# Block scaling and column shares of chunks three and four on VectorE instead of GpSimd, in a planned DeltaNet and SwiGLU kernel

## Chip, core and metric

The kernel runs on one core of one Trainium2 chip. The metric is the device time of one execution in microseconds, as the median of three runs.

## What is computed

The reference is a DeltaNet recurrence over 768 time steps for 4 batches and 8 heads of width 48, followed by an RMS norm and a SwiGLU feed-forward on the 3072 tokens of width 384 (inner width 1536):

```python
k_n = k / (np.linalg.norm(k, axis=-1, keepdims=True) + 1e-06)
for t in range(S):
    kt, vt, bt = (k_n[:, :, t], v[:, :, t], beta[:, :, t, None])
    y[:, :, t] = np.einsum('bhd,bhde->bhe', q[:, :, t], state)
    v_old = np.einsum('bhde,bhd->bhe', state, kt)
    state = state + bt[:, :, :, None] * np.einsum('bhd,bhe->bhde', kt, vt - v_old)
...
rms = np.sqrt(np.mean(x * x, axis=-1, keepdims=True) + 1e-06)
xn = x / rms * rms_g
g = xn @ w_gate
silu = g * (1.0 / (1.0 + np.exp(-g)))
val = xn @ w_val
return (silu * val @ w_out).astype(np.float32)
```

The weights arrive as 64-bit floats and are converted to 32 bits in the kernel.

## The kernel before

Time is cut into 12 chunks of 64 steps (`NCH`; `c` counts from 0, so the third and fourth chunk are `c = 2` and `c = 3`). Inside a chunk the recurrence needs the inverse of a unit triangular matrix of size 64 per head. `prep(c)` builds it from 32 x 32 blocks, 128 of them side by side, one per partition:

- the products of the keys (L537) are copied to SBUF (L634), stored to DRAM (`dkk`) and loaded back in another layout, one block per partition (`at`, L645);
- `scale` (L651) multiplies `at` by beta, a 128 x 1024 operation with two SBUF inputs;
- `share1` (L676), `share3` (L686, two small ones) and `share2` (L681) add to each odd column its share of the even one before it;
- 15 steps on VectorE (L698 multiply, L704 reduce) substitute forward two columns at a time in `acc`;
- the result is spread by copies (L721 on ScalarE, from the third chunk on also L725 on GpSimd), goes through DRAM (`dx`, `dxt`) and comes back as `mt`, `x2bd` and `m1bd`; two small products (L780, L804) finish `mt`.

For the first two chunks (`early`) the scaling and the shares run on VectorE, for the other ten on GpSimd; that is what `eng, e_` in L595 chooses. GpSimd also does the power operations (L559, L991, L992) and the scaling of keys (L626).

`recur(c)` then does the recurrence of a chunk: products on the state (L845), with the residual by VectorE (L859), `mt` times residual (L891), copied to `u` by VectorE (L930) and ScalarE (L928), then L905 and L942, sums (L973, L1044), the norm (L979 to L1007) and the transposes L1013. The feed-forward of the first two chunks (`ffn_plain`) has 12 column blocks in four passes, 24 in all: two products per block (L1080), Silu on ScalarE (L1087), the multiplication on VectorE that also empties the PSUM bank (L1088), and the product down (L1062). From the third chunk on `ffn` uses 15 products per half in place of 18 (L1173, L1183 to L1190) and a down product of the same kind (L1230). These need sums of weights, which VectorE makes once (L1136, L1138, L1209) after the 18 weight loads have been converted (L464 on ScalarE, L452, L455, L460 and L485 on VectorE).

Nothing of this is issued in the order of the code. Every piece is an operation of `Plan`: an engine, a duration, a priority, and the keys that it reads and writes. `Plan.run` plays the operations forward with these durations, and backward for new priorities, 60 times with some random shaking, and issues the order of the best round: each engine's queue is then fixed, and the engines meet only in semaphores. `op.port` (L87) makes the plan keep VectorE and GpSimd operations on SBUF apart. DMAs have a release time `after` in the plan, before which it doesn't start them; it is used in planning only. Up to 70 us of the plan, `filler` puts matmuls on a spare bank (L1330) where PE would stand idle. A changed duration, engine or release time can so change the order of every engine.

Of the kernel before, what the change touches and what calls it, by code (L numbers as in the profile page):

```python
# [248 lines left out]
def kernel(  # L249
# [17 lines left out]
    nc = tc.nc  # L267
# [24 lines left out]
    bk = sbt("bk", [128, W])  # L292
# [13 lines left out]
    NK, NKQ = 3, 2  # L306
    k2 = sbt("k2", [128, 16, DP], NK)
    q2 = sbt("q2", [128, 16, DP])
    vt = sbt("vt", [128, 16, D])
# [14 lines left out]
    acc = sbt("acc", [128, 4, W // 2, W])  # L324
# [21 lines left out]
    raw = [more[:, 1536 * i : 1536 * i + 1536].bitcast(I64) for i in range(NRAW)]  # L346
# [11 lines left out]
    P = Plan()  # L358
# [5 lines left out]
    def dma(dst, src, prio, r=(), w=(), work=0.3, dur=0.5, eng="SP", after=0.0):  # L364
        queue = nc.scalar if eng == "ACT" else nc.sync
        op = P.add(eng, dur, lambda: queue.dma_start(out=dst, in_=src), prio, r, w, lat=0.7)
        op.dma, op.work, op.ready = True, work, after
# [55 lines left out]
    def weights():  # L423
        todo = []
        for half_ in range(2):
            c0 = half_ * WCOL

            for i_ in range(3):
                for side, (key, w) in enumerate((("wg", moe_w_gate), ("wv", moe_w_val))):
                    c1 = c0 + 256 * i_  # L430
                    src = w.rearrange("(t p) c -> p t c", p=128)[:, :, c1 : c1 + 256]
                    todo.append((w_in[:, side, half_, i_:9:3], src, [(key, half_, i_)]))
                if i_:
                    for f in ((6 * half_,) if i_ == 1 else (6 * half_ + 2, 6 * half_ + 4)):
                        src = moe_w_out[f * 128 : f * 128 + 256, :].rearrange("(a p) c -> p a c", a=2)
                        z = spot(f)
                        todo.append((wo_sb[:, z : z + 2], src, [("wo", f), ("wo", f + 1)]))
        for n, (dst, src, keys) in enumerate(todo):
            pr = (30 if n < 9 else CV2) + 0.2 * n
            i, a = n % NRAW, n % NCV  # L440
            parts = dst.shape[1]
            rdst = raw[i].rearrange("p (a c) -> p a c", a=parts)
            dma(rdst, src, (0.1 if n == 0 else 3 + 2 * n), w=[("raw", i)], dur=0.7, work=3.06, after=(7.5, 5.0, 19.2, 27.2, 18.7, 33.3, 47.0)[n] if n < 7 else 48.8)

            low, high = (raw[i].bitcast(U32)[:, w_ : w_ + 2 * WCOL - 1 : 2] for w_ in range(2))
            top, cc = cva[a], cvb[a]
            u = top.bitcast(U32)
            tiled = lambda t: t.rearrange("p (a n) -> p a n", a=parts)
            cak, cvk = [("cva", a)], [("o", 1)] if a else [("tmp", 1), ("tmp", 2)]

            def s2(u=u):
                nc.vector.tensor_scalar(out=u, in0=u, scalar1=3, scalar2=None, op0=ALU.logical_shift_left)  # L452

            def s4(u=u, cc=cc):
                nc.vector.tensor_scalar(  # L455
                    out=cc.bitcast(U32), in0=u, scalar1=0xFF800000, scalar2=None, op0=ALU.bitwise_and
                )

            def s5(low=low, cc=cc, by=2.0**-52):
                nc.vector.scalar_tensor_tensor(out=cc, in0=low, scalar=by, in1=cc, op0=ALU.mult, op1=ALU.mult)  # L460

            P.add("ACT", 0.84, lambda high=high, top=top: nc.scalar.activation(out=top, in_=high.bitcast(FP32), func=ACTF.Prelu, scale=2.0**-112, alpha=2.0**32), pr, r=[("raw", i)], w=cak)  # L464
            P.add("DVE", 0.57, s2, pr, w=cak)
            P.add("DVE", 0.57, s4, pr, r=cak, w=cvk)
            P.add("DVE", 0.96, s5, pr, r=[("raw", i)], w=cvk)
            done = []
            if n < NPE:
                for x_ in range(2):  # L470
                    ps = Group()
                    cut = slice(2 * x_, 2 + x_)
                    flat = slice(512 * x_, 512 + 256 * x_)
                    m = 512 - 256 * x_

                    def s6(ps=ps, top=top[:, flat], cc=cc[:, flat], m=m):
                        nc.tensor.matmul(ps.t[:, 0:m], ident, top, start=True, stop=False)
                        nc.tensor.matmul(ps.t[:, 0:m], ident, cc, start=False, stop=True)

                    P.add("PE", 0.0035 * m, s6, pr, r=cvk + cak + ["ident"], w=[("cvp", n, x_)], ps=ps, size=8)  # L480
                    done.append(("cv", n, x_))
                    P.add("ACT", A(m), lambda dst=dst[:, cut], ps=ps, m=m: nc.scalar.copy(dst, ps.t[:, 0:m].rearrange("p (a n) -> p a n", n=256)), pr, r=[("cvp", n, x_)], w=[done[-1]], last=ps)
            else:
                done.append(("cv", n))
                P.add("DVE", 0.97, lambda dst=dst, top=tiled(top), cc=tiled(cc): nc.vector.tensor_tensor(out=dst, in0=top, in1=cc, op=ALU.add), pr, r=cvk + cak, w=[done[-1]])  # L485
            for key in keys:
                ready.setdefault(key, []).extend(done)
# [4 lines left out]
    def load(c, what):  # L492
        t0 = c * C
        pk, pq, pv = ((-5, 1, 12), (5, 29, 36))[c] if c < 2 else (due(c, 150), due(c, 99), due(c, 70))
        for key, t, src, pr in (("k2", k2[c % NK], k, pk), ("q2", q2, q, pq)):
            for g in range(2):
                if key[0] not in what:
                    continue
                dst = t[64 * g : 64 * g + 64, :, 0:D]
                s = src.rearrange("b (y g) t e -> g t (b y) e", g=2)[g, t0 : t0 + C]  # L500
                dma(dst, s, pr, w=[(key, c % NK if key == "k2" else 0, g)], dur=0.7, work=1.02, eng="ACT" if c == 0 and g and key == "k2" else "SP", after=((0.0, 1.4, 0.0), (8.6, 25.0, 0.0))[c]["kqv".index(key[0])] if c < 2 else 56.8)
        if "v" in what:
            for bb in range(2):
                s = v[2 * bb : 2 * bb + 2, :, t0 : t0 + C, :].rearrange("p h t e -> t (p h) e")
                dma(vt[64 * bb : 64 * bb + 64], s, pv, w=[("v", bb)], dur=0.85, work=1.02, after=(30.4, 40.0)[c] if c < 2 else 60.0)

    def turn(src, dst, keys, r, pr, split):

# [73 lines left out]
    def prep(c):  # L582
        early = c < 2
        pr = 8.0 if c == 1 else due(c, 110)
        if c == 0:
            pr = 0.0
        pn = pr if early else due(c, 125)
        pd = pr + (1 if c else 0)
        pi = (1.0, 45.0)[c] if c < 2 else due(c, 80)
# [2 lines left out]
        kd = kn[:, :, 0:D]  # L592
        kkeys = kkeys_(c)
        ktk = [("kt", ikq, hv) for hv in range(2)]
        eng, e_ = (nc.vector, "DVE") if early else (nc.gpsimd, "POOL")  # L595
        kkd = lambda d: [("kka", ikk // 2, d), ("kkb", ikk, d)]
        kkall = kkd(0) + kkd(1)
        kp = [("k2p", c % NK)]
        if c == 0:
# [24 lines left out]
            pr = 6.0  # L624
# [6 lines left out]
        for d in range(2):  # L631
            dst = kk[ikk][:, :, d:16:2]
            src = lambda d=d, ps=ps: ps[d].t.rearrange("p (u i t) -> p i u t", u=8, i=2)
# [3 lines left out]
        for g in range(2):  # L637
            for i in range(2):
                r0 = 64 * g + W * i
                src = kk[ikk][r0 : r0 + W, i] if c else kraw[r0 : r0 + W, :, W * i : W * i + W]  # L640
# [7 lines left out]
        bkeys = [("beta", i) for i in range(8)]  # L648
# [1 line left out]
        def scale():  # L650
            eng.tensor_tensor(out=at_, in0=at_, in1=(bt if c else bk)[:, None, :].to_broadcast([128, W, W]), op=ALU.mult)  # L651

        P.add(e_, 1.27 if early else 2.4, scale, pi, r=bkeys if c else ["bk"], w=[("at", 0), ("at", 1)])

        def start():
            nc.scalar.copy(acc[:, 0:4:3].rearrange("p a i t -> p a (i t)"), zero[:, 0:1, None].to_broadcast([128, 2, 512]))
# [14 lines left out]
        x, xkeys = (xs_[c + 1], [("xs", c)]) if early else (xs_[0], ["acc"])  # L671
# [15 lines left out]
                    out=a1[:, 1 : 1 + 34 * 15 + 1 : 34], in0=a1[:, 0 : 34 * 15 + 1 : 34], in1=diag[0:64], op=ALU.mult  # L687
                )

        P.add(e_, 1.17 if early else 1.3, share1, pi, r=[("at", 0), ("at", 1)], w=xkeys)  # L690
        P.add(e_, 0.5, share3, pi, r=[("at", 0), ("at", 1)], w=["acc"])
        P.add(e_, 0.69 if early else 1.3, share2, pi, r=xkeys, w=[("at", 0), ("at", 1)])
        for j in range(0, W - 2, 2):
            n, m = j // 2 + 1, W - 2 - j

# [32 lines left out]
        for par in range(2):  # L728
            dst = dx[i2].rearrange("i g x (s two) t -> two (i g x) s t", two=2)[par]
# [3 lines left out]
            dst = dxt[i2].rearrange("t g x s -> (g x) t s")[:, :, 16 * par : 16 * par + 16]  # L733
# [3 lines left out]
        for i in range(2):  # L737
            for bb in range(2):
                r0 = 64 * bb + W * i
                for g in range(2):  # L740
                    src = dx[i2][i, g, 8 * bb : 8 * bb + 8].rearrange("x s t -> s x t")
                    dma(mt[imt][r0 : r0 + W, 8 * g : 8 * g + 8, W * i : W * i + W], src, pi, r=xk, w=[("mt", imt, i, bb, g)], eng=next(turns))
        for y_ in range(4):
            src = dx[i2][1].rearrange("g (b y) s t -> y s (g b) t", y=4)[y_]
            dst = x2bd[W * y_ : W * y_ + W, :, y_]
            dma(dst, src, pi, r=xk, w=[("x2bd", y_)], eng=next(turns))
        if early:
# [13 lines left out]
            for g in range(2):  # L761
                s = slice(64 * g, 64 * g + W)
                for bb in range(2):
                    src = lambda s=s, bb=bb: psm[bb].t[s, 0:256].rearrange("p (x s) -> p x s", s=W)
                    dst = m1bd[s, 8 * bb : 8 * bb + 8, g]
# [4 lines left out]
        else:  # L770
            for g in range(2):
                src = dxt[i2][:, g]
                dst = m1bd[64 * g : 64 * g + W, :, g]
# [39 lines left out]
        for bb in range(2):  # L813
            s = slice(64 * bb, 64 * bb + W)
            dst = mt[imt][s, :, W:C]
# [548 lines left out]
```

## Time and profile before

| what | value |
|---|---|
| median of 3 runs | 717.94 us (716.83 to 719.15) |
| profiled execution | 717.62 us |
| its span, first to last instruction | 715.9 us |
| mean granted TensorE clock | 0.995 |
| L651 on GpSimd, 10 times | median 2370 ns |
| L651 on VectorE, 2 times | 1217 ns each |
| L676 on GpSimd, 10 times | median 1760 ns |
| L676 on VectorE, 2 times | 1127 ns each |
| first L1080 of PE | starts at 72.1 us |

Engines are PE (TensorE matmuls), PEld (its weight loads), DVE (VectorE), ACT (ScalarE), POOL (GpSimd) and SP (SyncE, which issues most DMAs). A line of the timeline gives start and duration in microseconds, the engine, the line of the code, the operation, the tiles (out<-in), the shapes and how many instructions are merged. A bracket at the end is idle time of the engine just before, with what ended it. "issue" there means that the profile names no releaser. All times count from the start of the span.

### The profile page before, as it was taken

How to read it: one execution, taken by the hardware profiler on the slowest of the kernel's cores; microseconds unless marked ns; L12 is line 12 of the kernel's file. 1: busy time of each engine (PE TensorE's matmuls, PEld its weight loads, DVE VectorE, ACT ScalarE, POOL GpSimd, SP SyncE). 2: the span in 40 equal slices, each digit the busy share in tenths (PEclk: the TensorE clock that was granted, in tenths of full speed). 3: DMA queues.
4: the chain of work that ended last, by engine and by line, in shares of the span. 5: the costliest groups of instructions: out<-in, count | busy, mean ns of one | idle time of the engine just before them, and what ended most of it. 6: DMA issues, size and time to landing. Idle time of an engine off the chain costs nothing.

```text
span 715.9 us, 23619 instructions
## 1 busy us (share of the span) xinstructions
PE 702.8 (98%) x10218; PEld 653.9 (91%) x10218; DVE 548.9 (77%) x1128; ACT 313.2 (44%) x732; POOL 150.3 (21%) x150
## 2 busy tenths in 40 slices
PE   9999999998999999999999999999999999999997
PEld 8898878766889999999999999999999999999997
DVE  4799887997969929948949959937959949957473
ACT  5435552432335435445446435346345354345231
POOL 4201123114132223114042130406042103000000
PEclk9999999998999999999999999999999999999999
DMA  7968794541261162162261252163160152040000
GB/s 139 247 122 187 190 238 97 125 83 24 45 119 26 30 113 47 23 112 55 38 121 35 40 99 46 25 108 75 21 116 14 24 99 45 16 62 2 23 2 22
DMA packets 210071, 54.68 MB, mean 76 GB/s; under 512 B 199216, under 2 KB 202288, under 8 KB 209968
## 3 DMA queue, kind: packets, MB, share of 16 engines
q1 hardware_dynamic: 205120, 52.26, 36.6%
q10 hardware_dynamic: 4848, 0.92, 0.9%
q8 instruction: 80, 1.31, 0.8%
q14 instruction: 23, 0.19, 0.1%
HBM read 40.83 MB, written 12.32 MB: 74 GB/s over the span
## 4 chain that ended last, share of the span: by engine, by line
PE 81%; DVE 11%; DMA 3%; POOL 2%; issue 2%; SPq 0%; ACT 0%; ACTq 0%; POOLq 0%; DVEq 0%
PE bank L1173 38%; PE bank L1230 19%; PE bank L1080 4%; PE bank L537 3%; PE bank L845 3%; DVE acc L704 2%; PE bank L514 2%; PE bank L1062 2%; DVE acc L698 2%; PE bank L905 2%; DMA more<-in_moe_w_val_dram 2%; PE bank L891 2%; PE bank L1330 2%; PE bank L804 1%; PE bank L942 1%
## 5 line engine op out<-in xcount | busy, mean ns | idle before, releaser
L1183 DVE TENSOR_TENSOR tmp<-tmp,bank 128x512 f32<-128x512 f32 x180 | 121.2, 683 | 92.2 <-PE bank L1173 74.6
L1173 PE MATMUL bank<-xf,w_in 128*128 128x128 f32 x1440 | 181.8, 277 | 0.0
L1173 PEld LDWEIGHTS bank<-xf,w_in 128*128 128x128 f32 x1440 | 170.7, 192 | 2.3 <-issue 0.6
L1173 PE MATMUL bank<-xf,more 128*128 128x128 f32 x960 | 124.6, 278 | 0.2 <-DVE tmp L1183 0.2
L1173 PEld LDWEIGHTS bank<-xf,more 128*128 128x128 f32 x960 | 115.0, 192 | 2.4 <-DVE tmp L1183 0.5
L1185 ACT COPY tmp<-bank 128x512 f32<-128x512 f32 x120 | 68.6, 584 | 72.9 <-PE bank L1173 56.0
L1189 ACT ACTIVATE tmp<-tmp 128x256 f32<-128x256 f32 x120 | 50.0, 418 | 91.7 <-DVE tmp L1183 91.4
L704 DVE TENSOR_REDUCE acc<-acc 128x30 f32<-128x90 f32 (+4 forms) x180 | 85.1, 473 | 6.2
L698 DVE TENSOR_TENSOR acc<-acc,at 128x60 f32<-128x60 f32 (+4 forms) x180 | 63.6, 353 | 7.7 <-POOL at L681 5.0
L1230 PE MATMUL bank<-wo_sb,hf 128*128 128x192 f32 x360 | 63.4, 327 | 0.0
L1190 DVE TENSOR_TENSOR hf<-tmp 128x256 f32<-128x256 f32 x120 | 55.6, 476 | 9.0 <-ACT tmp L1189 8.1
L1230 PEld LDWEIGHTS bank<-wo_sb,hf 128*128 128x128 f32 x360 | 58.2, 190 | 0.2
L559 POOL TENSOR_TENSOR knrm<-ksum,half 128x16 f32<-128x16 f32 x12 | 36.1, 3012 | 76.9 <-DVE ksum L558 76.9
L651 POOL TENSOR_TENSOR at<-at,beta_b 128x1024 f32<-128x1024 f32 x10 | 25.1, 2510 | 128.0 <-DMA at<-dkk 112.3
L725 POOL COPY acc<-acc 128x128 f32<-128x128 f32 x40 | 18.7, 496 | 129.3 <-DVE acc L704 128.8
L1330 PE MATMUL bank<-ident 128*128 128x128 f32 x338 | 44.0, 288 | 1.4 <-POOL ident masks.py:199 1.4
L1330 PEld LDWEIGHTS bank<-ident 128*128 128x128 f32 x338 | 41.6, 202 | 2.2 <-POOL ident masks.py:199 1.4
L1062 PE MATMUL bank<-wo_sb,hf 128*128 128x384 f32 x96 | 35.9, 510 | 1.1 <-DVE hf L1088 1.1
L1080 PE MATMUL bank<-xf,w_in 128*128 128x256 f32 x144 | 34.0, 383 | 0.0
L1080 PE MATMUL bank<-xp,w_in 128*128 128x256 f32 x144 | 32.9, 381 | 0.0
L1080 PEld LDWEIGHTS bank<-xp,w_in 128*128 128x128 f32 x144 | 27.0, 190 | 4.6
L1080 PEld LDWEIGHTS bank<-xf,w_in 128*128 128x128 f32 x144 | 26.6, 190 | 4.8 <-issue 0.2
(164 smaller groups left out, 1032.6 us busy)
## 6 DMA issues: line engine op xcount, KB each, us to landing
at<-dkk SPq DMA_DIRECT2D x23, 256.0 KB, 4.3
q<-in_q_dram SPq DMA_DIRECT2D x24, 192.0 KB, 3.6
more<-in_moe_w_val_dram SPq DMA_DIRECT2D x6, 768.0 KB, 5.6
more<-in_moe_w_gate_dram SPq DMA_DIRECT2D x6, 768.0 KB, 7.2
more<-in_moe_w_out_dram SPq DMA_DIRECT2D x6, 768.0 KB, 7.7
vt<-in_v_dram SPq DMA_DIRECT2D x24, 192.0 KB, 4.2
out_dram<-tmp SPq DMA_DIRECT2D x48, 96.0 KB, 2.2
k<-in_k_dram SPq DMA_DIRECT2D x23, 192.0 KB, 4.4
```

Of the source, the lines that this page charges most:

```text
L559: P.add("POOL", 2.95, lambda: nc.gpsimd.tensor_tensor(out=knrm[i2], in0=ksum[i2], in1=half, op=ALU.pow), pn, r=[("ksum", i2), "half"], w=[ ...
L698: nc.vector.tensor_tensor(out=acc[:, 1:3, 0:n, j + 2 : W].rearrange("p a i t -> p i a t"), in0=acc[:, old, 0:n, j : j + 2, None].to_broadc ...
L704: nc.vector.tensor_reduce(out=acc[:, new, 0:n, j + 2 : W], in_=acc[:, lo : lo + 3, 0:n, j + 2 : W].rearrange("p a i t -> p i t a"), axis=A ...
L1062: nc.tensor.matmul(po[p].t[:, 0:DM], hf[:, spot(f), 128 * p : 128 * p + 128], wo_sb[:, spot(f)], start=(f == f0), stop=(f == f1 - 1), skip ...
L1080: nc.tensor.matmul(ps.t[:, TOK * side : TOK * side + TOK], w_in[:, side, h_, 3 * t + i_, n : n + 128], x_[:, 2 * t : 2 * t + 2].rearrange( ...
L1173: nc.tensor.matmul(g.t[:, 128 * z : 128 * z + 128], fac[:, side, 128 * f : 128 * f + 128], xf[:, xs], start=(begin and z == 0), stop=False ...
L1183: P.add("DVE", V(512), lambda t=t, g=g: nc.vector.tensor_tensor(out=t, in0=t, in1=g.t, op=ALU.add), -1, r=[g], w=[tk], last=g)
L1185: P.add("ACT", A(512), lambda t=t, g=g: nc.scalar.copy(t, g.t), -1, r=[g], w=[tk], last=g)
L1189: P.add("ACT", A(256), lambda t=t: nc.scalar.activation(out=t[:, 0:256], in_=t[:, 0:256], func=ACTF.Silu), -1, w=[tk])
L1190: P.add("DVE", V(256), lambda t=t, f0=f0, p=p: nc.vector.tensor_tensor(out=hf[:, spot(f0) : spot(f0) + 2, 128 * p : 128 * p + 128], in0=t[ ...
L1230: nc.tensor.matmul(g.t[:, 0:192], a_[:, f], b_[:, f], start=(begin and f == 0), stop=(f == 5), skip_group_check=True)
L1330: nc.tensor.matmul(warm[:, 0:128], ident, ident)
```

## The change

The choice between the two engines is made by a new flag, `fast`, which is true for the first four chunks; the other uses of `early` stay. So L651, L676, L686 and L681 of the third and fourth chunk are issued to VectorE. The planned durations of these four follow the flag, and that of `share1` on GpSimd is now 1.7 where it was 1.3, that of `share3` on VectorE 0.3 where it was 0.5. The release times of five kinds of loads in the plan are others: the fifth weight load, the second chunk's q, the first chunk's v, and k and q of the later chunks. From L596 on the lines of the new kernel are two further down.

```diff
-  after=(7.5, 5.0, 19.2, 27.2, 18.7, 33.3, 47.0)[n] if n < 7 else 48.8)
+  after=(7.5, 5.0, 19.2, 27.2, 24.5, 33.3, 47.0)[n] if n < 7 else 48.8)
...
-  after=((0.0, 1.4, 0.0), (8.6, 25.0, 0.0))[c]["kqv".index(key[0])] if c < 2 else 56.8)
+  after=((0.0, 1.4, 0.0), (8.6, 27.2, 0.0))[c]["kqv".index(key[0])] if c < 2 else 53.2)
...
-  after=(30.4, 40.0)[c] if c < 2 else 60.0)
+  after=(34.4, 40.0)[c] if c < 2 else 60.0)
...
-        eng, e_ = (nc.vector, "DVE") if early else (nc.gpsimd, "POOL")
+
+        fast = c < 4
+        eng, e_ = (nc.vector, "DVE") if fast else (nc.gpsimd, "POOL")
...
-        P.add(e_, 1.27 if early else 2.4, scale, pi, r=bkeys if c else ["bk"], w=[("at", 0), ("at", 1)])
+        P.add(e_, 1.27 if fast else 2.4, scale, pi, r=bkeys if c else ["bk"], w=[("at", 0), ("at", 1)])
...
-        P.add(e_, 1.17 if early else 1.3, share1, pi, r=[("at", 0), ("at", 1)], w=xkeys)
-        P.add(e_, 0.5, share3, pi, r=[("at", 0), ("at", 1)], w=["acc"])
-        P.add(e_, 0.69 if early else 1.3, share2, pi, r=xkeys, w=[("at", 0), ("at", 1)])
+        P.add(e_, 1.17 if fast else 1.7, share1, pi, r=[("at", 0), ("at", 1)], w=xkeys)
+        P.add(e_, 0.3 if fast else 0.5, share3, pi, r=[("at", 0), ("at", 1)], w=["acc"])
+        P.add(e_, 0.69 if fast else 1.3, share2, pi, r=xkeys, w=[("at", 0), ("at", 1)])
```

More of the change, by code (lines that the diff above doesn't have):

```diff
@@ L442, in weights @@
             rdst = raw[i].rearrange("p (a c) -> p a c", a=parts)
-            dma(rdst, src, (0.1 if n == 0 else 3 + 2 * n), w=[("raw", i)], dur=0.7, work=3.06, after=(7.5, 5.0, 19.2, 27.2, 18.7, 33.3, 47.0)[n] if n < 7 else 48.8)
+            dma(rdst, src, (0.1 if n == 0 else 3 + 2 * n), w=[("raw", i)], dur=0.7, work=3.06, after=(7.5, 5.0, 19.2, 27.2, 24.5, 33.3, 47.0)[n] if n < 7 else 48.8)
             low, high = (raw[i].bitcast(U32)[:, w_ : w_ + 2 * WCOL - 1 : 2] for w_ in range(2))
@@ L500, in load @@
                 s = src.rearrange("b (y g) t e -> g t (b y) e", g=2)[g, t0 : t0 + C]
-                dma(dst, s, pr, w=[(key, c % NK if key == "k2" else 0, g)], dur=0.7, work=1.02, eng="ACT" if c == 0 and g and key == "k2" else "SP", after=((0.0, 1.4, 0.0), (8.6, 25.0, 0.0))[c]["kqv".index(key[0])] if c < 2 else 56.8)
+                dma(dst, s, pr, w=[(key, c % NK if key == "k2" else 0, g)], dur=0.7, work=1.02, eng="ACT" if c == 0 and g and key == "k2" else "SP", after=((0.0, 1.4, 0.0), (8.6, 27.2, 0.0))[c]["kqv".index(key[0])] if c < 2 else 53.2)
         if "v" in what:
@@ L504, in load @@
                 s = v[2 * bb : 2 * bb + 2, :, t0 : t0 + C, :].rearrange("p h t e -> t (p h) e")
-                dma(vt[64 * bb : 64 * bb + 64], s, pv, w=[("v", bb)], dur=0.85, work=1.02, after=(30.4, 40.0)[c] if c < 2 else 60.0)
+                dma(vt[64 * bb : 64 * bb + 64], s, pv, w=[("v", bb)], dur=0.85, work=1.02, after=(34.4, 40.0)[c] if c < 2 else 60.0)
     def turn(src, dst, keys, r, pr, split):
```

## The prediction

> **What bounds the kernel now.** I read the page's busy table first, then the table of stages, then the waits of TensorE, then the timeline around the one place that stands out.
>
> ```profile
> PE 702.8 (98%) x10218; PEld 653.9 (91%) x10218; DVE 548.9 (77%) x1128; ACT 313.2 (44%) x732; POOL 150.3 (21%) x150
> ```
>
> TensorE (PE) is busy 98% of the span, so the end moves only with PE work removed, PE idle time or a slower PE clock. The diff adds and removes no matmul of the computation. What is left is idle time and clock. The table of stages (columns: length, busy us of PE, PEld, DVE, ACT, POOL, then clock, DMA share, GB/s) shows where:
>
> ```profile
> 120.00:150.00 30.00, 30.00 (x241) 23.01 (x241) 28.85 (x55) 10.81 (x23) 2.84 (x4) 1.00 0.49 95
> 150.00:160.00 10.00, 8.93 (x79) 6.55 (x78) 9.86 (x15) 2.90 (x7) 1.62 (x1) 1.00 0.41 87
> 160.00:164.00 4.00, 0.90 (x5) 0.45 (x3) 4.00 (x4) 0.65 (x2) 3.84 (x5) 0.95 0.00 0
> 164.00:170.50 6.50, 6.46 (x124) 4.72 (x124) 4.36 (x13) 1.22 (x2) 1.57 (x2) 0.51 0.02 4
> ```
>
> From 120 us on VectorE (DVE) is full (28.85 of 30) while PE still finds work; at 160 PE runs dry with DVE and GpSimd (POOL) both full, and afterwards PE works for 6.5 us at a clock of 0.51. The waits of PE name two waits here, and the only others over 0.5 us lie before 60 us, which the change leaves in order:
>
> ```profile
> PE bank L891 <- issue: 3.1, 1, 3.1
> PE bank L1062 <- DVE hf L1088: 1.1, 1, 1.1
> ```
>
> L891 is the first recurrence product of the third chunk. What it waits for is in the timeline (start, duration, engine, line):
>
> ```profile
> 158.05 0.69 DVE L1138 TENSOR_TENSOR more<-w_in 128x512 f32<-128x512 f32 x1
> 158.77 2.73 DVE L1138 TENSOR_TENSOR more<-more,w_in 128x512 f32<-128x512 f32 x1
> 161.42 2.19 DVE L1138 TENSOR_TENSOR more<-w_in 128x512 f32<-128x512 f32 x1
> 163.53 0.74 DVE L1088 TENSOR_TENSOR hf<-tmp,bank 128x256 f32<-128x256 f32 x2
> 166.24 0.56 DVE L930 COPY u<-bank 128x384 f32<-128x384 f32 x1 [1.97 <-PE bank L891]
> ```
> ```profile
> 158.05 2.86 PE L1080 MATMUL bank<-xf,w_in 128*128 128x256 f32 x12
> 164.04 2.29 PE L891 MATMUL bank<-r,mt 64*64 64x48 f32 x64 [3.14 <-issue]
> ```
> ```profile
> 158.38 2.56 POOL L651 TENSOR_TENSOR at<-at,beta_b 128x1024 f32<-128x1024 f32 x1 [26.18 <-DMA at<-dkk]
> 161.02 2.03 POOL L676 TENSOR_TENSOR acc<-at 128x512 f32<-128x512 f32 x1
> ```
>
> L891 writes a PSUM bank that an L1088 of DVE has to empty. That L1088 stands behind two weight sums (L1138), each of 0.69 us when alone and of 2.73 and 2.19 while POOL runs L651 and L676 of the fourth chunk. So POOL's scaling stops DVE, and DVE stops PE. Price of the place: waits of 1.07 + 3.14, and matmuls at the half clock: L891 2.29 against 1.15 at 95 us, four L1062 2.93 against 1.45, L905 1.72 against 1.15, together 3.2. Sum 7.4 us.
>
> **What the Trainium skill says.** "SBUF — State Buffer", section "SBUF: two separate sides": VectorE and GpSimd share a port pair under an exclusive lock, and an op with two SBUF inputs against a GpSimd op blocks for the whole instruction. The trace agrees (2.73 against 0.69). "TensorE: Matmul & The Clock Gate", section "What's actually happening": about 3.4 us of idleness, in a free-running window, takes the clock to half. Here 3.14 us of idle time did it; the 1.07 us did not. "GPSIMD Engine Reference", section "4.1 Engine selection": two-input elementwise work is some 2 times slower there. The rows for L651 agree: 2370 ns median on POOL, 1217 ns on DVE.
>
> **The change, part by part.** All durations are of the profiled execution (717.62 us, span 715.9, so 1.7 outside); the median of the runs is 717.94, and I subtract from that.
>
> *Removed:* L651, L676, L686, L681 on POOL for the third chunk (2.70 + 1.78 + 0.44 + 1.30 = 6.2 us from 106.73) and the fourth (2.56 + 2.03 + 0.90 + 1.30 = 6.8 us from 158.38). With them go their stops of DVE: at 108.05 L562 took 1.41 instead of 0.17, then DVE idled 3.33 us before L698, and 2.04 + 1.50 at the two L1138: 8.1 us.
>
> *Added:* the same ops on DVE, twice, at the durations of the first chunks: 1.22 + 1.13 + 2 × 0.14 + 0.69 = 3.3 us each, 6.6 in all. So DVE gains only some 1.5 us in total, and the question is what stands behind the added ops. The new program's order shows it: for the fourth chunk they stand just ahead of the sixteenth L1088, whose bank is the one that L891 takes, and of L930, which L905 needs. Before, L1138 sums stood there, and L930 came ahead of the steps.
>
> *The plan made anew.* DVE's sum from the start of the first L1088 (75.4 us before; I take 75.5), each instruction at its row's median: 30.2 us to the end of L563, which is ahead of the first moved L651. Before, 23.7 us of such rows up to the sixth L1088 took 28.3: 4.6 us of gaps (waits for L464, that is for ScalarE and the weight loads) and one stop by POOL. I take 4.1, as the L577 now next to that POOL op reads PSUM. L626 of POOL then falls on the moved L651: 1.25, the excess it cost at 75.68 (1.82 against 0.56) and at 113.08 (1.47 against 0.22). So all that follows stands at 75.5 + 5.35 = 80.85 plus its sum: the sixteenth L1088 (77.1) ends at 158.0, L930 (81.8) at 162.6. The weights of conversions 15 to 18 are loaded and passed through ScalarE ahead of need in the new order, so I add no gap. POOL's L725 copies cost next to nothing, as before (L455 0.65 instead of 0.56).
>
> PE's sum from its first L1080 at 72.14 (three L1080 1.30; two L1062 1.29; L845, L537, L756, L891, L905 1.1 each; L942 0.87; L780 0.65; L804 1.0; four L514 0.52; six L1013 0.82): 82.3 to the last L1080 ahead of L891. Before, such a sum was 0.9 short by the seventh block. I add 1.0 for L1013, which now reaches its rows before POOL's root and the scaling L1007 are done, and 0.8 for a bank wait at the tenth block: PE reaches L891 at 157.1. It waits 1.1 for the bank, works 1.1 + 1.3 (L891, half a block), is at L905 at 160.6 and waits 2.2 for L930. Losses: 1.0 + 0.8 + 1.1 + 2.2 = 5.1 against 7.4. No single wait reaches 3 us, so I leave the clock at full. Gain 2.3; comparing where the two sums stand after L905 gives 2.6. I take 2.4: **715.5 us**. As L905 waits for DVE either way, waits ahead of it only trade places.
>
> *DMAs.* SyncE issues in order. Weight loads move ahead of the third chunk's dxt and dx stores, and the fourth chunk's dkk stores ahead of x2bd and mt. The load of `at`, issued at 153.8 and landed at 158.2 before, then goes out near 146 and lands near 150, 4 us before DVE reaches L651. If that cover were gone, DVE would stand still with L1088 behind it, one for one. Both ends for it: 0 to 2 us.
>
> *The rest.* Up to 70 us the fillers hide the new order; DVE's first two chunks keep theirs. After 170 us the waits of PE name none over 0.2 us, and POOL keeps the scaling from the fifth chunk on. The order of the last 30 us is nearly the same. I price this at 0, bounds -0.5 and +1.5, since a fresh order may hold a wait of its own.
>
> **Rivals.**
>
> *All of it goes* (710.5). If DVE's gaps before 110 us are 2 to 3 us smaller, both waits vanish with the clock loss: 717.9 - 7.4. For it: the weights are fetched earlier. Against: DVE's rows alone are full, and its added work precedes the bank's release.
>
> *Exchanged* (717.9). DVE is 2.4 us later than my sum, the clock stays full: what POOL took, DVE takes. For it: the waits for L464 hang on loads at a DMA share near 1.0 at 100 us. Against: the lock is really gone.
>
> *Clock drops again* (720.7, slower). Place: L891 and L905 of the third chunk, with the 3.3 us of moved ops ahead of the L1088 that frees the bank. If that L1088 ends after about 160.2, 2 us later than my sum, PE's wait at L891 reaches 3 us, the length that halved the clock before; price 3.2 on top of the 2.0: 717.94 - 2.4 + 2.0 + 3.2. Against: my waits are 1.1 and 2.2, with 2.4 us of work between.
>
> That the ops are not moved is excluded: the order shows them on DVE.
>
> **How the numbers follow.** 0.3% is 2.15 us, about what a measurement of this kernel can tell from no change. Forecast 0.42 (its own range 713.5 to 717.5; 0.27 of it faster), all of it 0.20 (faster), exchanged 0.20 (0.14 same, 0.04 faster, 0.02 slower), clock 0.18 (0.15 slower, 0.03 same). Faster 0.51, same 0.32, slower 0.17. The range reaches from the full gain, 710.3, to 720.5, which takes in nearly all of the exchange and the start of the clock case.
>
> **What would show it.** L651 with four instances on DVE at about 1.22 us and eight on POOL; L1138 at 0.69 with none over 1 us; the sixteenth L1088 ending near 158 and L930 near 162.6; PE waits at L891 and L905 of the third chunk near 1.1 and 2.2; clock 1.00 from 150 to 180. Wrong: a half-clock stretch there, a DVE wait for the DMA of `at`, or a PE wait over 1 us after 180 us.

## The result, and the profile after

| | median | runs | ratio to before |
|---|---|---|---|
| before | 717.46 us | 8 (716.03 to 719.15) | |
| after | 713.66 us | 8 (712.83 to 715.68) | 0.9958 (95%: 0.9939 to 0.9976) |

The medians are now of eight executions each. The ratio is estimated from the runs together with its interval, and is not the quotient of the two medians (0.9947). By the ratio the change gains 0.42% (0.24 to 0.61), about 3.0 us; between the medians it is 3.8. The forecast was 2.4. Where a gain is given "by the ratios" below, it is a difference of ratios times 717.5 us. The profiled execution took 713.07 us, its span is 711.3 (before: 717.62 and 715.9).

The table of stages of the changed kernel (length, busy us of PE, PEld, DVE, ACT, POOL, then clock, DMA share, GB/s):

```profile
120.00:150.00 30.00, 30.00 (x246) 23.45 (x245) 29.07 (x56) 9.67 (x22) 2.90 (x4) 1.00 0.48 93
150.00:160.00 10.00, 10.00 (x143) 7.58 (x141) 9.62 (x22) 4.21 (x9) 0.00 (x0) 1.00 0.33 55
160.00:164.00 4.00, 3.15 (x133) 2.42 (x132) 3.83 (x9) 0.27 (x1) 0.00 (x0) 1.00 0.01 4
164.00:170.50 6.50, 6.50 (x147) 5.15 (x146) 6.33 (x15) 1.64 (x6) 3.89 (x3) 1.00 0.33 63
```

VectorE is as full as before, but TensorE is now busy for 3.15 of the four microseconds at 160 us instead of 0.90, GpSimd is idle from 150 to 164, and the clock stays at 1.00 where it was 0.51. PE's waits over 0.7 us, after the wait for its first operand (us in total, how many, the longest):

```profile
PE bank L907 <- issue: 1.3, 1, 1.3
PE bank L782 <- DVE m1bd L771: 1.3, 1, 1.3
PE bank L907 <- DVE u L932: 0.8, 1, 0.8
```

The first two end before 67 us, ahead of the place of the change; only the third is at it. The timeline of VectorE, then of PE, there:

```profile
152.88 1.21 DVE L653 TENSOR_TENSOR at<-at,beta_b 128x1024 f32<-128x1024 f32 x1
154.12 1.13 DVE L678 TENSOR_TENSOR acc<-at 128x512 f32<-128x512 f32 x1
...
155.48 0.69 DVE L683 TENSOR_TENSOR at<-at,acc 128x512 f32<-128x512 f32 x1
156.09 0.41 DVE L1090 TENSOR_TENSOR hf<-tmp,bank 128x256 f32<-128x256 f32 x1
...
160.57 0.55 DVE L932 COPY u<-bank 128x384 f32<-128x384 f32 x1
```
```profile
157.69 1.15 PE L893 MATMUL bank<-r,mt 64*64 64x48 f32 x64
...
161.18 1.15 PE L907 MATMUL bank<-u,pt 64*64 64x48 f32 x64 [0.85 <-DVE u L932]
```

The sixteenth L1090 frees its bank at 156.50, and PE takes it at 157.69 without a wait. All L1140 take 0.68 to 0.69 us.

The waits that the profile lists are not all that PE loses. So I made a ledger, a sum of PE's lost time: for each matmul the time from its start to the next start, less the median of its line and shape in the kernel before, summed by stretch of the span. The part that all kernels share (some 43 us after 180, in most of them) says nothing; the differences do.

| PE's time over the medians, us | 0 to 80 | 80 to 150 | 150 to 180 | 180 to end | span |
|---|---|---|---|---|---|
| before | 14.9 | 7.5 | 9.7 | 43.8 | 715.9 |
| after | 16.9 | 8.1 | 4.3 | 42.4 | 711.3 |
| e1: order of before, both chunks on VectorE | 14.9 | 9.9 | 2.9 | 42.6 | 710.4 |
| e2: order of after, both on GpSimd | 16.1 | 11.7 | 5.2 | 42.6 | 715.1 |
| e3: numbers only | 19.3 | 14.5 | 2.7 | 48.8 | 725.7 |
| e4: old release times | 15.7 | 8.4 | 2.8 | 45.5 | 711.9 |
| e5: order of before, fourth chunk | 15.7 | 8.9 | 5.1 | 42.5 | 712.2 |
| e6: order of before, third chunk | 14.7 | 9.0 | 7.4 | 43.0 | 714.1 |
| e7: after, other seed | 14.8 | 10.4 | 4.4 | 41.5 | 710.6 |
| e8: before, other seed | 15.0 | 7.8 | 7.2 | 42.9 | 712.8 |
| e9: e8's order, both on VectorE | 14.6 | 7.7 | 3.3 | 42.3 | 708.2 |
| e10: order of before, all chunks | 15.9 | 7.6 | 3.4 | 43.9 | 710.8 |
| e11: release times only | 16.0 | 8.3 | 4.4 | 42.3 | 711.2 |
| e12: e11's order, both on VectorE | 15.5 | 12.4 | 4.1 | 43.2 | 715.2 |

From before to after, 5.4 us go at 150 to 180, 1.4 after 180, and 2.6 come back up to 150: 4.2, and some 0.5 more for four fewer fillers. Within the rounding that is the 4.6 of the spans. Each row is one execution: e1, e5, e6 and e10 have the very instructions and order of the kernel before up to 100 us, and yet their first column runs from 14.7 to 15.9; before and e5, the same up to 150 us, differ by 1.4 in the second. A difference of 1 in a single cell is no finding; that of 150 to 180 is several times larger, and the medians have the last word.

### The profile page after: what moved, and what is told of

Same layout as the page of the kernel before. It is cut to its first block, busy times and chain, and to the rows that moved or that the text cites. A ratio compares the mean times of both kernels' runs of the same rounds, so it can differ in the third digit from the quotient of the medians.

```text
span 711.3 us, 23614 instructions
## 1 busy us (share of the span) xinstructions
PE 699.6 (98%) x10214; PEld 651.5 (92%) x10214; DVE 545.1 (77%) x1138; ACT 312.2 (44%) x732; POOL 140.2 (20%) x140
## 4 chain that ended last, share of the span: by engine, by line
PE 80%; DVE 15%; DMA 1%; issue 1%; POOL 0%; ACT 0%; SPq 0%; ACTq 0%; DVEq 0%; POOLq 0%
PE bank L1175 38%; PE bank L1232 19%; PE bank L1082 4%; DVE acc L706 3%; PE bank L847 3%; PE bank L537 3%; DVE acc L700 2%; PE bank L514 2%; PE bank L1064 2%; PE bank L907 2%; PE bank L1332 2%; PE bank L893 2%; PE bank L806 1%; PE bank L944 1%; DMA at<-dkk 1%
## 5 line engine op out<-in xcount | busy, mean ns | idle before, releaser
L1175 PEld LDWEIGHTS bank<-xf,w_in 128*128 128x128 f32 x1440 | 170.9, 192 | 3.6 <-issue 0.8
L1192 DVE TENSOR_TENSOR hf<-tmp 128x256 f32<-128x256 f32 x120 | 51.6, 444 | 7.4 <-ACT tmp L1191 6.6
L1332 PE MATMUL bank<-ident 128*128 128x128 f32 x334 | 43.9, 289 | 1.4 <-POOL ident masks.py:199 1.4
L1332 PEld LDWEIGHTS bank<-ident 128*128 128x128 f32 x334 | 41.5, 203 | 2.2 <-POOL ident masks.py:199 1.4
L727 POOL COPY acc<-acc 128x128 f32<-128x128 f32 x40 | 22.5, 590 | 90.4 <-DVE acc L706 89.7
L653 POOL TENSOR_TENSOR at<-at,beta_b 128x1024 f32<-128x1024 f32 x8 | 18.9, 2366 | 106.5 <-DMA at<-dkk 92.1
L1082 PE MATMUL bank<-xf,w_in 128*128 128x256 f32 x144 | 34.6, 386 | 0.0
L1064 PE MATMUL bank<-wo_sb,hf 128*128 128x384 f32 x96 | 34.4, 492 | 0.0
L1241 DVE TENSOR_TENSOR tmp<-tmp,bank 128x192 f32<-128x192 f32 x30 | 10.5, 350 | 31.1 <-PE bank L1232 30.1
L1082 PE MATMUL bank<-xp,w_in 128*128 128x256 f32 x144 | 33.4, 381 | 0.0
L1082 PEld LDWEIGHTS bank<-xp,w_in 128*128 128x128 f32 x144 | 26.9, 190 | 4.9 <-DVE hf L1090 0.2
```

Source lines behind the costliest of these rows:

```text
L1064: nc.tensor.matmul(po[p].t[:, 0:DM], hf[:, spot(f), 128 * p : 128 * p + 128], wo_sb[:, spot(f)], start=(f == f0), stop=(f == f1 - 1), skip ...
L1082: nc.tensor.matmul(ps.t[:, TOK * side : TOK * side + TOK], w_in[:, side, h_, 3 * t + i_, n : n + 128], x_[:, 2 * t : 2 * t + 2].rearrange( ...
L1175: nc.tensor.matmul(g.t[:, 128 * z : 128 * z + 128], fac[:, side, 128 * f : 128 * f + 128], xf[:, xs], start=(begin and z == 0), stop=False ...
L1192: P.add("DVE", V(256), lambda t=t, f0=f0, p=p: nc.vector.tensor_tensor(out=hf[:, spot(f0) : spot(f0) + 2, 128 * p : 128 * p + 128], in0=t[ ...
L1332: nc.tensor.matmul(warm[:, 0:128], ident, ident)
```

## The experiments

Theory 1: GpSimd's scaling stops VectorE where VectorE is full, VectorE holds a bank that PE needs, and PE stands still and loses clock. Theory 2: what changed the time is the fresh order of the plan, not the engine. Each run has the line numbers of its own kernel: L1088 of the kernel before is L1089 where one line was added (e1, e5, e6, e9, e10, e12), L1090 in the changed kernel and L1091 in e2.

**The engine alone, and the order alone.** "Order kept" means that the plan is made with the old engine and durations, and only the instruction goes to another queue, at the same place in the order.

```diff
 # e1, in the kernel before, after the choice of eng
+        eng = nc.vector if c < 4 else nc.gpsimd
 # e2, in the changed kernel, at the same place
+        eng = nc.vector if early else nc.gpsimd
 # e3, in the changed kernel, planned anew
-        fast = c < 4
+        fast = c < 2
 # e4, in the changed kernel, planned anew: 18.7, 25.0, 30.4 and 56.8 in place of 24.5, 27.2, 34.4 and 53.2
```

> The order, durations and release times of the kernel before are kept; the four operations of the third and fourth chunk are only issued to VectorE, at the place in the order that the plan had for them on GpSimd. Theory 1 (the gain comes from GpSimd no longer stopping VectorE at the fourth chunk's scaling): no L1139 over 1 us, PE's wait before the first product of the third chunk falls from 3.1 us to under 1.5, no half clock at 164 us, and the head of the kernel before is kept, so 712 us (711 to 714). Theory 2 (the gain comes from the fresh order and the new numbers, not from the engine): 717 us or more, as the order is the old one.

Measured 710.78 us, ratio 0.9906 (0.9889 to 0.9923): the engine alone gains 6.7 us by the ratio, more than the whole change, and the time is just below the 711 to 714 of theory 1. VectorE and PE in e1:

```profile
159.02 0.68 DVE L1139 TENSOR_TENSOR more<-w_in 128x512 f32<-128x512 f32 x1
159.62 0.41 DVE L1089 TENSOR_TENSOR hf<-tmp,bank 128x256 f32<-128x256 f32 x1
159.95 1.22 DVE L652 TENSOR_TENSOR at<-at,beta_b 128x1024 f32<-128x1024 f32 x1
```
```profile
161.86 1.15 PE L892 MATMUL bank<-r,mt 64*64 64x48 f32 x64
```

The bank is free at 160.03, where it was 163.9 before; PE comes 1.8 us later and does not wait. 9.7 us of the ledger become 2.9.

> The order of the changed kernel is kept, and the four operations of the third and fourth chunk are issued to GpSimd as before. Theory 1: GpSimd takes 2.4 + 1.8 + 0.4 + 1.3 us where VectorE took 3.3, stops VectorE meanwhile, and the sixteenth L1091 stands behind it: PE waits 3 us or more at the third chunk's first product or copy, the clock halves there, 718 us or more. Theory 2: the order is the new one, so 713.7 us within 1.5.

Measured 718.04 us, ratio 1.0007 (0.9989 to 1.0025): the order of the change without its engine gains nothing. Theory 2 falls for this change. But the way was not the expected one. No L1141 near 153 us is stopped. In the fourth chunk VectorE instead waits for GpSimd to finish its slower scaling and shares, and PE for the copy behind the steps (L908). The stops are in the third chunk, and PE waits behind them at L848:

```profile
108.45 3.12 DVE L485 TENSOR_TENSOR wo_sb<-more 128x768 f32<-128x768 f32 x1
160.13 0.22 DVE L701 TENSOR_TENSOR acc<-acc,at 128x60 f32<-128x60 f32 x1 [3.80 <-POOL at L684]
```
```profile
PE bank L908 <- DVE u L933: 1.8, 1, 1.8
PE bank L848 <- DVE state L1047: 1.6, 1, 1.6
```

L485 takes 0.95 us in the changed kernel. The half clock came too, but at 119 us, for 3.41 us, after the wait at L848, and not at 164. L848 waits for a sum of VectorE (L1047) that stands behind the third chunk's scaling and shares (108 to 115 us on GpSimd).

> The changed kernel with its flag true for the first two chunks only: the five new release times and the duration of 1.7 for share1 on GpSimd, planned anew, with the third and fourth chunk on GpSimd. Theory 1: the stop of VectorE is back, 717.5 us within 2; a long L1140 and a PE wait of 2 to 3 us near 160 us. Theory 2 (the numbers and the fresh order): 714 us within 1.

Measured 726.28 us, ratio 1.0121 (1.0101 to 1.0141). Both theories missed it by over 8 us. The longest wait of PE is in the head, at an instruction that waits 1.0 to 1.4 us in the other kernels, and VectorE's idle time ahead of it is a wait for ScalarE:

```profile
PE bank L782 <- DVE m1bd L771: 5.4, 1, 5.4
```
```profile
54.37 0.56 DVE L452 TENSOR_SCALAR xf<-xf 128x768 uint32<-128x768 uint32 x1 [7.06 <-ACT xf L464]
53.42 0.92 ACT L464 ACTIVATE xf<-more 128x768 f32<-128x768 f32 x1 [6.71 <-DMA x2bd<-dx]
```

In this order L464 stands behind ScalarE's own issues of the first chunk's mt and x2bd, around which ScalarE idles for 6.7 us, and L452 waits for L464. VectorE stands still meanwhile, and behind L452 stand the second chunk's scaling and steps and the copies L771 that PE waits for. The head is only a part of the loss: by the ledger e3 loses 4.4 us more than the kernel before up to 80 us, 7.0 more from 80 to 150 and 5.0 more after 180. The 7.0 hold a wait of 2.5 us at L847 with a half clock behind it; the rest was not traced. At 150 to 180 e3 loses only 2.7: the stop there was not its trouble.

> The changed kernel with the old release times of the five kinds of loads, planned anew; the four operations stay on VectorE. Theory 1: 713.7 us within 1.5; if the 1.4 us that the changed kernel is late by at 75 us come from the new release times, 712.3. Theory 2: back to 717 us, since the release times made the good order.

Measured 713.75 us, ratio 0.9945 (0.9929 to 0.9961). The release times are not needed for the gain. Of the 2.0 us that the changed kernel loses up to 80 us, 1.2 are absent here, but 3.1 come back after 180 in an order of its own.

**One chunk at a time, and other seeds.**

```diff
 # e5 and e6, in the kernel before, order kept
+        eng = nc.vector if c < 2 or c == 3 else nc.gpsimd
+        eng = nc.vector if c < 3 else nc.gpsimd
 # e7 in the changed kernel, e8 in the kernel before
-        rng = random.Random(77)
+        rng = random.Random(78)
```

> The order of the kernel before, kept; only the fourth chunk's four operations are issued to VectorE, the third chunk's stay on GpSimd. Theory 1 (the stop of VectorE at the fourth chunk's scaling sets the time): no wait at the third chunk's first product L892, none of the 1.7 us of new PE waits at 105 to 113 us that moving both had, a small wait of under 1 us at L906: 710.5 us within 1. A rival (the third chunk's stop of 4.6 us, which makes VectorE late for all that follows, is the cause): half or more of the loss stays, 714 us or more.

Measured 713.35 us, ratio 0.9949 (0.9935 to 0.9962), 2.9 us above what theory 1 gave and 0.7 below its rival's 714. No wait is left at L892, but two others are:

```profile
PE bank L1063 <- DVE hf L1089: 1.0, 1, 1.0
...
PE bank L906 <- DVE u L931: 0.9, 1, 0.9
```

The first stands in the kernel before too (L1062, 1.07 us, up to 152.2) and neither in e1 nor in e6, where the third chunk is on VectorE: it belongs to the third chunk's operations on GpSimd. What these cost VectorE, 4.6 us in the kernel before, is mostly not a stop: 1.2 of it is L562 (1.41 instead of 0.17), and the rest is VectorE waiting for GpSimd's result:

```profile
113.08 1.47 DVE L698 TENSOR_TENSOR acc<-acc,at 128x60 f32<-128x60 f32 x1 [3.33 <-POOL at L681]
```

So theory 1 is too narrow: GpSimd delays VectorE by stopping it and by being slower at work that VectorE needs. The change of engine takes both away, and no run separates them. L1063 and L906 together leave 5.1 us at 150 to 180 where e1 has 2.9, which is about the difference of the two spans (1.8).

> The order of the kernel before, kept; only the third chunk's four operations are issued to VectorE. Theory 1: two L1139 stay long (2.7 and 2.2 us) and the bank of L892 comes free 3.5 us later than with both moved, at 163.5 us, while PE is there at 161.9: a wait of 1.7 us without a half clock, 712.5 us; if PE's wait still reaches 3 us the clock halves again and it is 717. The rival (third chunk is the cause): 711 us with no long wait.

Measured 714.36 us, ratio 0.9969 (0.9956 to 0.9982). The wait was 3.0, not 1.7: PE was there at 160.8, a microsecond earlier than in e1's execution, and GpSimd starts when `at` lands, at 158.0 (158.4 in the kernel before):

```profile
158.49 2.73 DVE L1139 TENSOR_TENSOR more<-more,w_in 128x512 f32<-128x512 f32 x1
161.14 2.19 DVE L1139 TENSOR_TENSOR more<-w_in 128x512 f32<-128x512 f32 x1
163.25 0.74 DVE L1089 TENSOR_TENSOR hf<-tmp,bank 128x256 f32<-128x256 f32 x2
```
```profile
163.76 2.35 PE L892 MATMUL bank<-r,mt 64*64 64x48 f32 x64 [2.98 <-issue]
```

The same two stops and the same wait, with the half clock 3.41 us long instead of 6.83. So each chunk has a part: by the ratios 3.7 us for the fourth (e5), 2.2 for the third (e6), 6.7 for both (e1). "The fourth chunk alone" was wrong.

> The changed kernel with another seed for the random shaking of the plan, so another order of all engines with the same engines and numbers. Theory 1: the four operations are on VectorE, so no stop at 150 to 170 us whatever the order: 713.5 us within 3, below the kernel before. Theory 2 (an order that happened to be good): anywhere, as likely above 717.5 as below.

Measured 714.10 us, ratio 0.9956 (0.9942 to 0.9970), as theory 1 had it.

> The kernel before with another seed for the shaking of the plan: another order, with the third and fourth chunk on GpSimd. Theory 1: GpSimd's scaling falls again on the stretch where VectorE is full, and stops it by some 3 us per chunk; if it falls ahead of an L1090 that PE waits for, 717.5 us within 3, otherwise down to 713. Theory 2: another order is worth several us either way.

Measured 714.27 us, ratio 0.9959 (0.9947 to 0.9972): with GpSimd still scaling, another seed of the plan gains as much as the change. Both theories allowed it, so the time alone decides nothing. The trace shows the stops in full, on other instructions:

```profile
156.76 2.52 DVE L1138 TENSOR_TENSOR more<-w_in,more 128x512 f32<-128x512 f32 x1
159.19 2.24 DVE L1138 TENSOR_TENSOR more<-w_in 128x512 f32<-128x512 f32 x1
```
```profile
164.66 1.53 PE L905 MATMUL bank<-u,pt 64*64 64x48 f32 x64 [2.26 <-DVE u L930]
```

The L1088 with the bank of L891 stood ahead of them this time, so one shorter wait is left, with 3.41 us of half clock behind it.

**Does the engine bring the same in every order?**

```diff
 # e9: e8 with the engine changed, order kept. e10: before, order kept, all chunks
+        eng = nc.vector if c < 4 else nc.gpsimd
+        eng = nc.vector
 # e11: before with the five new release times, planned anew. e12: e11 with the line of e9, order kept
```

> The kernel before with the other seed of the run e8_before_seed (714.3 us), its order kept, and the four operations of the third and fourth chunk issued to VectorE. Theory 1 as it now stands (GpSimd's stops of both chunks make VectorE late, whatever the order): no L1139 over 1 us, the wait of 2.3 us before L906 and the half clock of 3.3 us after it go, 710 us (708.5 to 711.5). Theory 2 (a good order had already taken the gain): 714 us, or more if the moved operations land badly.

Measured 712.28 us (709.36 to 715.18), ratio 0.9924 (0.9896 to 0.9952): 2.5 us below e8 by the ratios, but 0.8 above the range of theory 1, and spread widely. The trace is of one of the faster executions (709.9); why two others took 715 is not known. In it L906 starts at 161.98 without a wait, L931 having ended at 159.9, and no half clock follows: 3.3 us at 150 to 180 against e8's 7.2.

> The order of the kernel before, kept; the four operations of all twelve chunks are issued to VectorE. Theory 1: from 180 us on PE waits nowhere over 0.2 us, so taking GpSimd's stops away there brings nothing: the same as with only the third and fourth chunk, 710.8 us within 1. If the stops matter in the steady part too, 708 us or less; if VectorE lacks the room there, 713 us or more.

Measured 711.47 us, ratio 0.9912 (0.9896 to 0.9929), the same as e1 within the intervals: in the eight later chunks, where no wait of PE in the kernel before exceeds 0.2 us, GpSimd's work costs nothing that these runs can tell, and VectorE has the room.

> The kernel before with only the five new release times, planned anew; engines and durations as before. With these and the longer share1 on GpSimd it was 726.3 us, 8.5 above the kernel before, losing up to 80 us, from 100 to 150 us and after 400 us. If the release times made that bad order: 724 us or more. If the duration of 1.7 for share1 did: 717.5 us within 2.5.

Measured 713.63 us, ratio 0.9940 (0.9921 to 0.9959), below both expectations. So e3's bad order came with the planned durations (1.7 for share1 on GpSimd, 0.3 for share3), the only other thing in which it differs; which of the two was not tried. And the release times alone gain as much as the whole change. GpSimd, VectorE and PE in e11:

```profile
153.79 5.14 POOL L651 TENSOR_TENSOR at<-at,beta_b 128x1024 f32<-128x1024 f32 x1 [20.79 <-DMA at<-dkk]
```
```profile
156.02 3.45 DVE L1138 TENSOR_TENSOR w_in<-w_in,more 128x512 f32<-128x512 f32 x2
159.40 0.41 DVE L1088 TENSOR_TENSOR hf<-tmp,bank 128x256 f32<-128x256 f32 x1
```
```profile
160.13 1.15 PE L891 MATMUL bank<-r,mt 64*64 64x48 f32 x64
```

`at` lands more than 4 us earlier, GpSimd is held off for more than half of its 5.14 us, and then stops VectorE once; the bank is free at 159.81, 0.3 us before PE needs it. The stop is there and covered, in this execution by 0.3 us.

> The kernel of e11_releases_only (713.6 us), its order kept, with the four operations of the third and fourth chunk issued to VectorE. In e11 GpSimd's scaling still stopped VectorE (the L1138 at 156 us took 2.74), but the L1088 behind it ended at 159.8, before PE came for its bank at 160.1: no PE wait hung on the stop. Theory 1 in its sharp form (a stop costs only what a PE wait shows, so an order that covers it leaves nothing to gain by the engine): 713 us within 1. A rival (the engine is worth 4 us or more in every order): 709.5 us or less.

Measured 713.49 us, ratio 0.9944 (0.9924 to 0.9964), as expected: where the order covers the stop, the engine brings nothing that can be told from noise (+0.3 us by the ratios, 2 either way). The rival's 4 us or more is excluded. Its profiled execution, 716.96, is the longest of its eight; it holds a wait of 2.18 at L537, at 113 us, and a half clock after it, which are not of this place.

## Why the prediction was right, and where it was not

What the engine is worth depends on the order it is done in. The last column is by the ratios; its "±" is an estimate from the two 95% intervals, added in squares.

| order | on GpSimd | on VectorE | engine, us |
|---|---|---|---|
| of before | 1 | 0.9906 (e1) | -6.7 ± 1.2 |
| of after | 1.0007 (e2) | 0.9958 | -3.5 ± 1.9 |
| other seed | 0.9959 (e8) | 0.9924 (e9) | -2.5 ± 2.2 |
| new release times | 0.9940 (e11) | 0.9944 (e12) | +0.3 ± 2.0 |

The first value stands apart from the other three; 2.5 and 0.3 can't be told apart.

- *The cause* was right: GpSimd's scaling delays VectorE, and that is worth what PE waits behind it. e1 moved the operations with the order held and gained 6.7 us; e2 put them back on GpSimd and lost the gain. The prediction counted all 8.1 us that VectorE lost as stops; 3.33 of them are the wait for GpSimd's result shown under e5. That the change brings less is due to its fresh order: at the same engines, after is 3.7 us above e1 (0.9958 against 0.9906). The ledger shows 2.0 of it up to 80 us and 1.4 at 150 to 180, and 1.8 in favour of after between; where all of it lies stays open.
- *The gain* was 3.8 (3.0 by the ratio) and not 2.4. The mis-sized term is VectorE's sum. I added row durations, and from L563's end to the sixteenth L1090 that made 46.9 + 1.25 us. It took 45.9 (110.58 to 156.50). There, 44 of 83 instructions begin before the one ahead has ended, by 0.08 us each, 3.5 in all, while gaps between the others add only 1.3: an L1140 of 0.680 is followed by the next after 0.602. L563 itself ended 0.8 us later than summed (110.6 against 109.8): the first L1090 started at 76.9 and not 75.5, and the gaps up to there were 3.6 and not 4.1. So L1090 ended at 156.5 and not 158.0, L932 at 161.1 and not 162.6, and the waits of 1.1 and 2.2 became 0 and 0.85. (By the prediction's own times they come to 0.9 and 2.0: each has 0.2 us that it does not name.) The Trainium skill says why ("Perfetto Trace Analysis", section "DVE / Act Engine Instruction (TENSOR_ADD, Activation, etc)"): the profiler's end is the acknowledged write, and the next instruction may begin to read before. Elapsed time has to be taken from start to start.
- *Waits of PE ahead of L893.* The 1.0 at L1013 and the 0.8 at the tenth block are not there; L1015 at 106.96 and the blocks after it follow without one.
- *The head* was priced at 0 (-0.5 to +1.5 with the rest), and cost: the first L1082 starts at 73.66 instead of 72.14. The order of after loses 16.5 us up to 80 us (16.9, and 16.1 in e2), that of before 15.2 (mean of before, e1, e5, e6, e10): 1.3 us. With the old release times (e4) it is 15.7, so they may have a part; e7, with the new ones and another seed, has 14.8, so it isn't they alone. This miss and the one in VectorE's sum go against each other, so that the forecast came as near as it did is partly luck.
- *The lock of L626 on the moved scaling* was right in size. VectorE got there first by 0.2 us, so it was `share1` (L678) that paid: 2.29 us instead of 1.13, an excess of 1.16 against 1.25 forecast. VectorE, then GpSimd:

```profile
110.50 1.16 DVE L653 TENSOR_TENSOR at<-at,beta_b 128x1024 f32<-128x1024 f32 x1
111.69 2.29 DVE L678 TENSOR_TENSOR acc<-at 128x512 f32<-128x512 f32 x1
```
```profile
110.71 2.27 POOL L628 TENSOR_TENSOR k<-k,krec 128x768 f32<-128x768 f32 x1 [1.56 <-PE bank L944]
```

- *The clock* stayed full, as forecast. Its price of 3.2 us was that of one execution. The mean granted clock of 55 executions of the kernel before was 0.9969, against 0.995 in the profiled one, 0.9985 in 8 of after and 0.9996 in 5 of e1. As an estimate, (1 - clock) x span makes that 2.2 us before, 1.1 after and 0.3 in e1, the program's end included. Of the gain, the clock then has some 1.1 us in after and 1.9 in e1, and the waits the rest. The same estimate gives 3.4 us for the profiled execution, so the 7.4 was some 1.2 too high for a usual execution of before.
- *DMAs*: VectorE does not wait for the third or fourth chunk's `at`, as forecast.
- *The rivals.* Exchanged and the clock case did not come: VectorE was not later but earlier than summed, and no wait reached 1 us there. All of it goes came close at the place itself, where 5.4 of the 7.4 us went by the ledger; but 2.6 came back ahead of it, which that rival did not name. The price of one mechanism was right, but the prediction took the order as given. e8 and e11 gained 3 to 4 us with GpSimd in place, and e3 lost 8.7: the spread of orders is as large as what was to be predicted, and none of the rivals named that.

The fastest is e1, 710.78 us, below before (0.9906) and after (0.9958), with e10 the same within the intervals. It is an edit of one line that leaves the plan alone. On VectorE all six orders that ran for these two chunks lie between 0.9906 and 0.9958; on GpSimd five lie between 0.9940 and 1.0121.

## What to carry to other kernels

A delay of one engine by another costs what the bound engine waits behind it, so look first for what the delayed engine holds; in the later chunks, with PE hardly waiting, GpSimd's work was free. When an order is planned, run the engine change in the old order and the new order with the old engine: only then is the gain the change's own, and here the plain swap beat the fresh plan by 3.7 us. Add up a busy engine from start to start, not by durations.

## What the runs showed of the hardware

- The half clock came in stretches of 3.41 us (e2, e6, e8, e12, and twice in e3) or of 6.83, twice that (before). In each of these traces the start of a stretch and the start of the half clock at the program's end lie a whole number of 3.413 us apart: 162 times in before, 174 in e2, 194 and 177 in e3, 161 in e6, 160 in e8, 176 in e12. That fits the free-running window that the prediction took from the Trainium skill ("TensorE: Matmul & The Clock Gate", section "What's actually happening"). Its 3.4 us of idleness do not fit as the length of a wait. In the kernel before, the half clock began 2.68 us into the wait at L891. Waits of 2.26 (e8), 2.18 (e12) and 1.60 (e2) stood ahead of one too, while one of 1.80 (e2, at L908) did not. Nor does a longer wait bring a longer half clock: 3.14 gave two windows, 2.98 (e6) and 5.45 (e3) gave one. So "no single wait reaches 3 us" was no safe bound.
- An instruction of VectorE that reads a PSUM bank was not stopped: in e2 an L1091 at 155.91 took 0.42 us, as elsewhere, inside GpSimd's L654 (152.72 to 156.52), while in the kernel before the sums L1138, which read SBUF alone, took 2.73 and 2.19 instead of 0.69.
- Some waits of PE fall in the middle of a group of like matmuls and have no releaser:

```profile
113.37 0.73 PE L537 MATMUL bank<-qt,kt 64*64 64x64 f32 x33 [2.18 <-issue]
```

  This one is from e12. The 14 traces hold 19 such waits of over 0.4 us. In all of them a 16 KB packet of the DMA queue that the profile marks "instruction" had ended 1.2 to 1.6 us before PE went on (111.79 and 113.37 here); most packets of that queue bring no wait. That PE waited for its instructions is an inference; no run tested it.
